# One attention-and-gate kernel: the order of its first loads and casts, and the queue of its output stores

## The chip, the cores and the metric

The kernel runs on one core of one Trainium2 chip. The metric is the device time of one execution in microseconds (us). Thirteen executions of the kernel before took 387.77 to 391.29 us, with a median of 389.75 us.

The engines are called as in the profile: PE is TensorE (PEld its weight loads), DVE is VectorE, ACT is ScalarE, POOL is GpSimd, and SP is SyncE, which only issues DMAs. DMAs issued by SP and ACT go to hardware queues (q1 and q10 in the profile), those issued by POOL to a software queue (q0).

## What is computed

```python
# q, k, v: (8 batches, 12 heads, 448 rows, 64), f32
scores = (1 / 8) * q @ k.T
m = max(scores); e = exp(scores - m)
x = (e / (sum(e) + exp(-m) + 1e-9)) @ v          # heads side by side: (8, 448, 768)
proj = x @ w_proj                                # (768, 2304), cut into x1, x2, x3
x2c = irfft(rfft(x2, axis=rows) * rfft(filter))  # filter: (448, 768)
out = (x1 * x2c * x3) @ w_out                    # (8, 448, 768), f32
```

The kernel computes in bf16 on PE. It leaves out the subtraction of the maximum, so that the denominator is the sum of exp plus 1, and it writes the two Fourier transforms as products with small cosine and sine tables.

## The kernel before

**Units of work.** Heads go in pairs: a batch has six pairs, and pair numbers run through the whole kernel. Pairs 0 to 5 are batch 0, pairs 6 to 11 batch 1, and so on to pair 47. Below, q8 is the query load of pair 8, k8 and v8 its key and value loads.

**Attention of a pair** (`attention`, from L650). Score products (L662 and L664) fill a PSUM tile `sc`, ACT takes the exponential of four tiles (L670 three times, L675 once), PE multiplies by the values in two halves (L707, L712), and DVE divides (L725 to L727) into `xb`. Then the result is turned, on PE in batches 0 and 1 (L761), into `xT`.

**The gate part of a batch** (`dense`) folds `xT` into `xf` on DVE (L822, L827), multiplies it by the middle third of `w_proj` (task P, L850), transforms it (task Z, L877), multiplies `xT` by the two other thirds (task G, L923), transforms back (task I, L962), and multiplies by `w_out` (task O, L1035). ACT copies each result of O into a ring of three tiles `osb` (L1047), and a DMA stores it (`store`, L1051). The filter's spectrum (L607, L614, L617, L624) is made once, in batch 0.

**How batches 0 and 1 get their inputs** (`staged`, L300). For each pair there is a key load, a value load and two query loads (one for each head), all f32, into one of four slots of `nat`. With them go four loads called rests, which hold the last 64 rows of keys and values of all heads. SP issues all of them but q0, in one order. A load must wait until the slot's last user has been cast. POOL casts to bf16: keys at L343, queries at L349, values at L356, rests at L372 and L377. Then PE turns keys and queries of the pair (L384 to L390; call this task T), and DVE, or ACT for pair 6, copies them into `kT` and `qT`. The casts of keys and queries write rings of two tiles, so that the key cast of pair 8, for example, must wait until T of pair 6 has run.

**How batches 2 to 7 get theirs** (`loaded`, L432). POOL issues DMAs that cast on the way (L441, L449, L451 and L463), and SP issues DMA transposes (L475, L480, and L751 for the attention's result).

**The weights and the filter** also come by POOL's software queue: the middle third of `w_proj` first, then the filter, the first third, the last third, and `w_out` (L555 to L559, L640, L645).

**What sets the order.** Nothing runs in the order of the code. Each step is a task with an engine, a cost, a due time, and the names of what it needs and makes. `Plan.run` plays the tasks through in a model of its own, and each engine always takes the most urgent task that is ready there. The program then holds the instructions of each engine in that order, and each engine runs them strictly in it. Three rules of the plan matter here:

- SP takes a load only if at most nine are under way with it; a query load counts as two (L128).
- A weight load becomes ready when the loads named in `GATES` (L210) have been issued, or their casts done. This exists in the plan alone: in the built program the first weight DMA waits for no semaphore and has only its place among POOL's instructions.
- The due times of values, rests and casts come from `tau`, which gives each pair of batch 0 a slot of 3.5.

The softmax here doesn't subtract the row's maximum and nothing guards it: scores larger than these inputs give would overflow.

## Time and profile before

| what | us |
|---|---|
| median of 13 executions (lowest to highest) | 389.75 (387.77 to 391.29) |
| the profiled execution's own time | 387.77 |
| its span, first to last instruction | 386.0 |
| PE busy in the span | 370.0 |
| DVE, ACT, POOL busy | 269.7, 264.3, 113.3 |
| moved by DMA | 50.44 MB, mean 131 GB/s |

Busy times are of one profiled execution. An engine's time without work counts only where the engine is the one that everything else waits for. The number after a group's x is how many instructions it has, and a bracket at a line's end says how long the engine was idle before it and what ended that.

The DMA queues of the profile count packets. For a load, a packet is one contiguous run: a query load's runs are 256 bytes, those of a key or value load 768 bytes.

### The profile page before, as it was taken

What the parts mean: (1) busy time and instruction counts of PE and PEld (TensorE: products, weight loads), DVE (VectorE), ACT (ScalarE), POOL (GpSimd) and SP (SyncE); (2) the same over time, 40 slices, a digit from 0 to 9 for tenths busy, and PEclk for the clock granted to TensorE, in tenths of its full rate; (3) what the DMA queues carried; (4) which work ended last, traced back from release to release, by engine and by line L of the source; (5) the groups of instructions that cost most, each with busy time, mean ns of one, the idle gap of its engine ahead of it and who ended that gap; (6) DMA issues with size and microseconds to landing.
All of it is one profiled execution on the core that took longest, in us unless ns stands there. A gap on an engine that the chain in (4) does not pass through costs nothing.

```text
span 386.0 us, 8977 instructions
## 1 busy us (share of the span) xinstructions
PE 370.0 (96%) x3461; PEld 232.7 (60%) x3461; DVE 269.7 (70%) x817; ACT 264.3 (68%) x460; POOL 113.3 (29%) x179
## 2 busy tenths in 40 slices
PE   6877999999999999999999999999999999999995
PEld 5554765656665566556756576556655566567652
DVE  6587669862987459956698439956699439964870
ACT  6788676737876757866877768766876758743543
POOL 7775828237241713331406222322100000000000
PEclk9899999999999999999999999999999999999999
DMA  8999999999999999799999699799951321012004
GB/s 202 244 251 230 213 206 176 149 123 226 145 141 126 221 163 137 88 110 167 149 119 87 145 171 136 88 107 160 120 70 30 122 56 29 15 54 84 0 2 164
DMA packets 179419, 50.44 MB, mean 131 GB/s; under 512 B 166125, under 2 KB 175792, under 8 KB 179376
## 3 DMA queue, kind: packets, MB, share of 16 engines
q0 software_dynamic: 101680, 17.80, 64.5%
q1 hardware_dynamic: 76768, 31.83, 42.5%
q8 instruction: 27, 0.44, 0.5%
q10 hardware_dynamic: 928, 0.23, 0.3%
q14 instruction: 16, 0.13, 0.1%
HBM read 43.86 MB, written 11.01 MB: 142 GB/s over the span
## 4 chain that ended last, share of the span: by engine, by line
PE 82%; DVE 7%; DMA 5%; ACT 2%; SPq 2%; issue 1%; POOL 0%; POOLq 0%
PE pps L923 24%; PE pps L850 15%; PE ops L1035 13%; PE op L712 8%; PE sc L662 7%; DMA wproj_bf<-in_moe_w_proj_dram 3%; PE op L707 3%; PE xsp L877 3%; PE cps L962 3%; DMA nat<-in_q_dram 2%; PE sc L664 2%; PE sc L923 1%; PE sc L850 1%; SPq L321 1%; DVE cv L991 1%
## 5 line engine op out<-in xcount | busy, mean ns | idle before, releaser
L670 ACT ACTIVATE e<-sc 128x896 bf16<-128x896 f32 x144 | 127.5, 923 | 17.2 <-PE sc L662 16.0
L923 PE MATMUL pps<-xT,wproj_bf 128*128 128x448 bf16 x522 | 110.6, 352 | 0.1
L923 PEld LDWEIGHTS <-wproj_bf 128*128 128x128 bf16 x576 | 52.0, 97 | 45.8 <-issue 5.9
L850 PE MATMUL pps<-wproj_bf,xf 128*113 128x384 bf16 x360 | 66.7, 328 | 1.0 <-DMA wproj_bf<-in_moe_w_proj_dram 0.8
L850 PEld LDWEIGHTS <-xf 128*113 128x113 bf16 x384 | 48.6, 132 | 16.4 <-issue 5.5
L712 PE MATMUL op<-vn,e 128*128 128x65 bf16 x1152 | 57.0, 194 | 0.0
L712 PEld LDWEIGHTS <-e 128*128 128x128 bf16 x1152 | 50.6, 98 | 5.2
L1035 PE MATMUL ops<-wout_bf,yT 128*128 128x384 bf16 x270 | 49.2, 326 | 0.1
L449 POOL DMA_DIRECT2D nat<-in_k_dram x36 | 29.8, 845 | 48.2 <-DMA kT<-nat 47.2
L727 DVE TENSOR_TENSOR xb<-op,rec 128x256 bf16<-128x256 f32 x96 | 40.7, 424 | 3.3
L707 PE MATMUL op<-vr,er 128*128 128x130 bf16 x192 | 42.2, 220 | 0.7 <-DVE xb L727 0.7
L725 DVE TENSOR_SCALAR rec<-op 128x4 f32<-128x4 f32 x96 | 15.2, 158 | 39.6 <-PE op L712 38.5
L662 PE MATMUL sc<-qT,kT 64*128 64x448 bf16 x288 | 40.9, 357 | 0.6 <-DVE qT L410 0.5
L1047 ACT COPY osb<-ops 128x384 f32<-128x384 f32 x52 | 24.2, 484 | 22.9 <-PE ops L1035 22.6
L1035 PEld LDWEIGHTS <-yT 128*128 128x128 bf16 x288 | 26.5, 98 | 20.0 <-DVE yT L1006 2.5
L891 DVE TENSOR_TENSOR t<-xs,hrs 113x768 bf16<-113x768 bf16 (+1 forms) x64 | 34.2, 552 | 5.6 <-ACT xs L885 5.4
L675 ACT ACTIVATE er<-sc 128x448 bf16<-128x448 f32 x48 | 26.7, 555 | 14.2 <-PE sc L664 13.5
L862 DVE CAST x<-pps 113x384 bf16<-113x384 f32 x32 | 17.7, 554 | 25.0 <-PE pps L850 24.9
L971 ACT CAST cr<-cps 128x452 bf16<-128x452 f32 x48 | 26.0, 550 | 9.4 <-PE cps L962 9.2
L938 DVE TENSOR_TENSOR g<-x,pps 128x448 bf16<-128x448 bf16 x45 | 27.8, 617 | 6.7 <-PE pps L923 6.4
L935 ACT CAST x<-pps 128x448 bf16<-128x448 f32 x42 | 23.0, 547 | 13.6 <-PE pps L923 12.6
L885 ACT CAST xs<-xsp 113x384 bf16<-113x384 f32 (+1 forms) x60 | 26.5, 490 | 3.8 <-PE xsp L877 3.2
(117 smaller groups left out, 463.7 us busy)
## 6 DMA issues: line engine op xcount, KB each, us to landing
out_dram<-osb SPq DMA_DIRECT2D x24, 384.0 KB, 2.4
nat<-in_q_dram POOLq DMA_DIRECT2D x24, 168.0 KB, 7.0
vn<-in_v_dram POOLq DMA_DIRECT2D x6, 672.0 KB, 11.0
wproj_bf<-in_moe_w_proj_dram POOLq DMA_DIRECT2D x3, 1152.0 KB, 12.1
nat<-in_k_dram POOLq DMA_DIRECT2D x36, 96.0 KB, 4.1
nat<-in_q_dram SPq DMA_DIRECT2D x22, 112.0 KB, 5.1
nat<-in_k_dram SPq DMA_DIRECT2D x12, 192.0 KB, 4.6
nat<-in_v_dram SPq DMA_DIRECT2D x12, 192.0 KB, 4.7
```

The lines of the kernel that those rows point to most:

```text
L449: nc.gpsimd.dma_start(kn[:, :, 1 + t, c], kr[:, :, 4 * u + t, :])
L662: nc.tensor.matmul(sc[:, u, 0:S], kT[b % 2][c, hp, t, :], qT[b % 2][c, hp, :])
L670: nc.scalar.activation(e[:, 0 : 2 * S].rearrange("p (u n) -> p u n", u=2), sc[:, :, 0:S], AF.Exp, scale=SCALE)
L675: nc.scalar.activation(e[:, 0:S], sc[:, 0, 0:S], AF.Exp, scale=SCALE)
L707: nc.tensor.matmul(op[:, n, :, :], e[0][:, o : o + 128], vr[b % 2][:, hp, :, :], start=True, stop=False)
L712: nc.tensor.matmul(op[:, n, u, :], e[1 + t][:, u * S + o : u * S + o + 128], vn[b % 2][:, hp, 4 * u + t, :], start=False, stop=(u == 1 and ...
L727: nc.vector.tensor_tensor(W["xb", b][:, hp, 2 * hf : 2 * hf + 2, :].rearrange("p t (u d) -> p t u d", u=2), op[:, :, :, 0:DH], rec[:].unsq ...
L850: nc.tensor.matmul(pps[:FQ, :DCH], W["xf", b][:, pg, kt, 0:FQ], wproj_bf[:, kt, D + ch * DCH : D + (ch + 1) * DCH], start=(kt == 0), stop= ...
L891: nc.vector.tensor_tensor(t[:K], L["xs", par, ch][:K], h, op=ALU.mult)
L923: nc.tensor.matmul(p[:, :S], wproj_bf[:, kt, 2 * part * D + dt * 128 : 2 * part * D + (dt + 1) * 128], xT()[:, kt, 0:S], start=(kt == 0), ...
L938: nc.vector.tensor_tensor(g[:, dt, :], L["x1", dt], p[:, :S], op=ALU.mult)
L1035: nc.tensor.matmul(ops[:n, :DCH], y[:, dt, 0:n], wout_bf[:, dt, ch * DCH : (ch + 1) * DCH], start=(dt == 0), stop=(dt == NDT - 1),)
```

## The change

Five edits of the plan's inputs, and one of the program:

1. The value loads of batch 0 are due 3.5 later in the plan (`VLATE`), and the rests of the values of batch 0 are due 0.4 later.
2. The two casts of batch 1's key rests are due 12.0 ahead of pair 6 instead of 5.9 (`CRK`).
3. The middle third of `w_proj` may be loaded once the keys and queries of pair 6 have been issued, where it was pair 7.
4. `REV` is a name for what was done already, and `late` is an argument that no task uses.
5. The output stores of batches 0 to 6 are issued by POOL on the software queue, not by SP. Those of batch 7 stay with SP. In the plan a store costs its engine 1.0, where it was 0.6.

```diff
+    VLATE = 3.5
+    CRK = 12.0
+    REV = True
...
     GATES = (
-        (1, [("iv", 5), ("ir", 1), ("ik", 7), ("iq", 7)]), ("F", [("cv", 8)]), (0, [("cv", 9)]), (2, [("cv", 10)]),
-        ("O", [("cv", 11)]),
+        (1, [("iv", 5), ("ir", 1), ("ik", 6), ("iq", 6)]), ("F", [("cv", 8)]), (0, [("cv", 9)]), (2, [("cv", 10)]), ("O", [("cv", 11)]),
     )
...
-                add("ACT" if first else "SP", 1.04 if name == "q" else 0.52, -21.0 if first else want + 0.1 * n, load, need=need,
+                add("ACT" if first else "SP", 1.04 if name == "q" else 0.52, -21.0 if first else want + 0.1 * n + (VLATE if name == "v" and b == 0 else 0.0), load, need=need,
...
-                    add("SP", 0.5, want + (0.05 if name == "k" else SLOT0 + 0.05) if b == 0 else want - RE1 + 0.1 * n,
+                    add("SP", 0.5, want + (0.05 if name == "k" else SLOT0 + 0.45) if b == 0 else want - RE1 + 0.1 * n,
...
-                    add("POOL" if on_pool else "DVE", 0.55 if on_pool else 0.37, tau(g) - 5.9 if g else 3.0,
+                    add("POOL" if on_pool else "DVE", 0.55 if on_pool else 0.37, tau(g) - CRK if g else 3.0,
...
+            dma = nc.sync if b == n_batches - 1 else nc.gpsimd
             if st < 3:
-                nc.sync.dma_start(out[b, st * 128 : (st + 1) * 128, :], osb)
+                dma.dma_start(out[b, st * 128 : (st + 1) * 128, :], osb)
                 return
             for i in range(1 + b % 2):
-                nc.sync.dma_start(out[b - b % 2 + i, 384:S, :], osb[i * REM : (i + 1) * REM])
+                dma.dma_start(out[b - b % 2 + i, 384:S, :], osb[i * REM : (i + 1) * REM])
...
-                add("SP", 0.6, w, lambda: store(st), need=[("os", b, st)], make=[("store", b, st)], give=[os_], dma=1.4, run=3072)
+                add("SP" if b == n_batches - 1 else "POOL", 1.0, w, lambda: store(st), need=[("os", b, st)], make=[("store", b, st)], give=[os_], dma=1.4, run=3072)
```

The numbers of the plan move the order of the built program. These are the first DMAs that SP issues, in both orders (k, v and r are one DMA each, q is two; rk and rv are rests, with the batch's number). The number in brackets is the place of the DMA before it.

```
before: k0 rk0 v0 k1 rv0 q1 v1 k2 q2 v2 k3 v3 q3 k4 v4 q4 rv1 rk1 k5 [23] q5 v5 v6 q6 k6 [30] v7 k7 q7 v8 k8 [36] q8 v9 k9 k10 [41] q9 v10 v11 q10 k11 q11
after:  k0 rk0 k1 q1 v0 rv0 k2 v1 q2 k3 q3 v2 k4 v3 rk1 q4 rv1 k5 v4 [23] k6 v5 k7 v6 q5 [29] v7 k8 k9 q6 v8 v9 [36] q7 v10 k10 v11 [41] q8 k11 q9 q10 q11
```

On POOL, the casts around the first weight load (w1 is the middle third, w0 the first) stand so:

```
before: ... k5 q5 v5 | w1 | q6 rk1 rk1 k6 v6 k7 rv1 rv1 v7 q7 v8 | filter | q8 k8 k9 v9 | w0 | ...
after:  ... k5 v4 k6 v5 | w1 | v6 q5 rv1 rv1 v7 rk1 rk1 k7 q6 k8 v8 | filter | q7 v9 | w0 | q8 k9 ...
```

On PE, T of pair 7 and the first score product of pair 7 move from before the first P to behind it; T of pair 6 moves from before the last scores of pair 5 to behind pair 5's value products; between the first P and T of pair 8 there were one P and one pair of scores, and now there are T of pair 7, two P and one pair of scores. After batch 1 PE's order is the same but for three swaps of neighbours. On POOL each store stands between the loads of a later batch: those of batch 2, for example, among the first key loads of batch 5, and those of batch 3 from the last query load of batch 6 on.

## Prediction

> **What bounds the kernel now.** First the page's slices for PE, then the busy time of each engine in four stretches (columns: stretch, length, busy time and instructions of PE, PEld, DVE, ACT, POOL, then granted clock, DMA share, GB/s).

> ```profile
> PE   6877999999999999999999999999999999999995
> ```
> ```profile
> 0.00:35.50 35.50, 26.38 (x349) 18.58 (x350) 25.56 (x88) 27.10 (x40) 25.36 (x73) 0.95 1.04 234
> 35.50:50.15 14.65, 14.37 (x138) 10.06 (x138) 9.26 (x25) 10.92 (x22) 8.72 (x15) 1.00 1.12 210
> 50.15:360.00 309.85, 308.42 (x2845) 192.34 (x2843) 221.90 (x672) 215.88 (x379) 79.19 (x92) 1.00 1.16 121
> ```

> PE idles 9.1 us of the first 35.5 and 1.7 of the next 324.5. So the time is the head, then PE's own work, which the change leaves as it is, then the tail. An edit gains only by an earlier first P (35.50), and loses wherever PE comes to wait after it. In the head DMA is busy throughout. The chain of waits (start, length, what) passes the head through query landings and the first weight:

> ```profile
> 17.30 3.33 DMA nat<-in_q_dram
> 21.97 1.42 issue
> 23.40 12.06 DMA wproj_bf<-in_moe_w_proj_dram
> ```

> The timeline of POOL shows w1's place and the gap ahead of it, and the filter; that of PE shows the first P, which waits 0.79 us for w1, and T of pairs 8 and 10:

> ```profile
> 21.32 0.64 POOL L356 CAST vn<-nat 128x192 bf16<-128x192 f32 x2
> 23.40 1.07 POOL L640 DMA_DIRECT2D wproj_bf<-in_moe_w_proj_dram  x1 [1.43 <-DMA nat<-in_q_dram]
> ...
> 31.09 0.75 POOL L555 DMA_DIRECT2D filt<-in_moe_filter_fft_dram  x1
> ```
> ```profile
> 35.50 1.14 PE L850 MATMUL pps<-wproj_bf,xf 128*113 128x384 bf16 x6 [0.79 <-DMA wproj_bf<-in_moe_w_proj_dram]
> ...
> 38.07 0.22 PE L384 MATMUL tps<-ident_bf,ks 128*128 128x128 bf16 x1
> ...
> 55.91 0.22 PE L384 MATMUL tps<-ident_bf,ks 128*128 128x128 bf16 x1
> ```

> Last the DMA queues (packets, MB, share), for 30 to 31 us, while w1 lands, and for 40 to 41, between two weights:

> ```profile
> q0 software_dynamic: 112, 0.17, 94.3%
> q1 hardware_dynamic: 110, 0.03, 21.2%
> ```
> ```profile
> q1 hardware_dynamic: 610, 0.22, 95.7%
> q0 software_dynamic: 11, 0.00, 3.2%
> ```

> While a weight lands, the two queues take turns packet by packet: SP's loads get 110 packets a us, and 600 where the software queue is empty. A query DMA is 448 packets of 256 bytes, so it takes 448 / 110 = 4.1 us beside a weight, a key or value DMA 256 / 110 = 2.3. This is the price that decides below. The trace agrees: the last three loads of the head, k11 and both parts of q11, landed at 47.62, 51.70 and 55.95, 4.1 and 4.3 apart, under w0 and w2.

> **The change part by part.** All sums stand against the profiled execution (387.77, the lowest of the 13; the median is 389.75). Differences are then put on the median.

> *Edits 1 to 3, the first P.* The casts ahead of w1 are now k5, v4, k6, v5. Their loads are SP's DMAs 22 to 25, and the landings at these places were 18.95, 19.61, 19.81 and 20.62. With casts of 0.50 and 0.64 (rows at 20.11 and 21.32) they end near 21.4. With the gap of 1.43 kept, w1 is issued at 22.8, 0.6 earlier. The gap's releaser is given as a query load, but the instruction waits for no semaphore in the program; if it is a wait that goes, w1 gains 2.0, if POOL is later, 0. P also needs the fold of batch 0. q5 now lands as DMA 28/29 (22.21 and 23.05 at these places) and is cast after w1's issue, near 25.2. Then come T of pair 5, six exponentials (0.45 to 0.92 each, some 4.7), the values and the fold: 35.6, where before it was 35.95. So the first P ends near 36.1, 0.5 earlier. T of pair 7 (0.42) and one score product (0.19) now stand behind it: together +0.1. If the fold does not follow, +0.6; if w1 gains 2.0 and the fold with it, -1.4.

> *Edits 1 and 3, the later queries.* SP's order in places 28 to 43 has the same kinds in the same places as before, so landings can be carried over by place. But places 42/43, which were q9, are now q8, and places 45/46 and 47/48, behind k11, are q9 and q10. Before, q8 landed at 35.13, q9 at 41.77 and q10 at 43.67, and T of pairs 8, 9 and 10 ran at 38.07, 49.98 and 55.91. So q9 and q10 had slack of 8 and 12 us; it is this slack that the change spends. Two more things take it. The filter's issue now stands behind the key cast of pair 8, which must wait for T of pair 6, and that stands behind the values of pair 5: near 33.5 instead of 31.09. And w0 is issued right after v9's cast, near 36.6, where it was 39.86. Before, the software queue was empty from about 39.5 to 42.5, and in that gap q9, v10, v11 and q10 all came through (41.77 to 43.67). After, filter, w0, w2 and wout follow each other without a gap.

> The slowest DMA engine sets a landing. Each DMA's semaphore gets 16 increments, one for each engine, and their times for place 40 are:

> ```
> 34.3 34.5 34.5 34.6 34.6 34.6 34.6 34.7 34.7 34.7 34.8 34.8 35.6 35.7 37.5 38.7
> ```

> Fourteen engines were through before the filter's packets came at 35.1, two lagged 1 to 2 us behind after w1 and took the rest at the slow rate. On the slowest, place 38 was through at 35.1 (an earlier w1 does not help: what it leaves sooner it took sooner). At the fast spacing of 0.6 a DMA places 39 to 43 would be through at 38.1. The filter's first packets come 4.0 us after its issue (31.09 to 35.1), so now at 37.5: one query DMA is left for the slow rate, and **q8 lands near 38.1 - 0.6 + 4.1 = 41.6**. The other bounds are the rows of w1 (23.40 to 26.6, 3.2 us) and w0 (39.86 to 42.3, 2.4): with 2.4, packets at 35.9, nearly four DMAs left, q8 near 48. From the other side, if no engine lags, q8 is through near 36.5.

> From there the queue has k11, q9 and q10 to bring: 2.3 + 4 x 4.2 = 19.1 us beside the weights. Hence q10 at 60.7, cast (0.61) at 61.3. PE would come to T of pair 10 at 55.9, so **PE loses 5.4 us**, of which 3.1 at T of pair 8 (41.6 + 0.6 against 39.1, where PE stands after P, T of pair 7, two P and two score products) and the rest at T of pair 10. For T of pair 11 two more query DMAs give 69.1, cast 69.7 against 64.15 + 5.4: the same within 0.2. Bounds: no lag, 36.5 + 19.1 + 0.6 - 55.9 = +0.3; late, the weights' own end stops it. Filter (5.9 long) and three weights of 8.2 (w0's 42.3 to 50.7 less its start) from 35.9 end near 66.5, and then the rest is fast: q10 near 66.5, loss 11. I take 4.0, since it is the filter's own row. POOL, SP and PE are in order, so what stands behind the stalls shifts by the same, and the loads of batch 2, which queue behind wout, with it.

> *Edits 2 and 4* cost nothing of their own: the two key-rest casts (0.53 each) stand on POOL ahead of the key cast of pair 8, which has to wait for T of pair 6 in any case, so POOL's wait there hides them. If that cover went, +1.

> *Edit 5, the stores.* Each issue now costs POOL 0.7 to 0.95 us (rows of L449 and L441), 27 of them in 240 us on an engine that is 29% busy; loads of later batches slip by 9 to 14 us, covered by a wait of 47.2 us that POOL has at L449 for the key transposes. What can be felt is `osb`: in batches 1, 3 and 5 a fourth copy needs the first store landed (batch 3: copied 213.59, store 213.61 to 216.44, fourth copy at 219.63). The page's rows:

> ```profile
> out_dram<-osb SPq DMA_DIRECT2D x24, 384.0 KB, 2.4
> ...
> nat<-in_q_dram POOLq DMA_DIRECT2D x24, 168.0 KB, 7.0
> ```

> At 2.4 there are 3.2 us in hand, at 7.0 the copy comes about 1.6 late, three times. So 0 to 4.8; since POOL's queue is empty in those places (its loads were done), I take 0.2.

> [...]

> **Sum:** 0.1 + 5.4 + 0.2 = +5.7, so 393.5 for the profiled execution and **395.4 on the median**.

> The stalls of 3 us leave PE without work, and the row of 12.0 to 15.4 shows the clock granted at 0.50 after an idle time of 1.08 us: by it up to 1.7 us more, which is within the upper bound. [...]

> **The rivals** (on the median).
> - *Later still* (0.22): the filter's packets come 2.4 to 3.2 us after issue; q8 lands at 44 to 48, loss 7 to 11, 397 to 401. The filter's own row speaks against it.
> - *Little lost* (0.20): the slow engines lag by less, or the filter is issued later than 33.5, so that q8 is through near 38 and q10 near 57: +0.5 to +3, 390.9 to 392.7. It decides from the filter's packets: after 38.1 at T of pair 8 nothing is lost.
> - *No change* (0.10): the same with no lag at all, 389 to 390.9.
> - *Faster* (0.20), the other side: the gap of 1.43 is a wait for a query load that goes; w1 gains 2.0, PE's half-clock stretch at 12.0 to 15.4 goes as well since T of pair 1 has its keys and queries sooner, and the whole fold comes 1.4 to 2 earlier, while q8 is in time for the reason just given: 387 to 388.4. It decides if q10 is cast by about 54.5. For it: the chain passes this gap; against it: a wait that no semaphore of the program holds.
> - The forecast (0.28): 393 to 397.

> A change that does nothing is excluded by the two orders.

> **How the numbers follow.** About 0.3% (1.2 us) can be told from no change. Faster 0.20; within 0.3%: the case of no change and a part of "little lost", 0.14; slower 0.66. Range: from the faster case's end at 388.2 to 399.5 in the later one, which leaves about 0.1 out on each side.

> **What would show it.** w1's issue near 22.8 and the first P at 34.9 to 35.5; the filter's issue near 33.5, its packets 4 us later; q8 landed near 41.6, q10 near 60.7; PE's lines for T of pairs 8 and 10 with waits of 2 to 3 us each, for a query cast of POOL; no such waits at L1047 in batches 1, 3 and 5. It is wrong if the two slow DMA engines are not slow there, if w0's packets leave a gap after the filter, or if P starts before 34.5.

## The result and the profile after

The changed kernel took **394.27 us** (median of 11 executions, 392.50 to 399.05), the kernel before 389.89 us (48 executions, 387.73 to 394.84): a ratio of **1.0117**, 95% interval 1.0096 to 1.0138, so 4.4 us slower. Ratios and intervals, here and below, are of the executions in the faster of two states alone (399.05 is of the slower), and so are not the quotients of the medians beside them. The prediction had 395.4. Its sign and its size held, but the places where the time goes are not the ones it named, as the profile shows.

The page of the changed kernel, the rows of PE and of the granted clock in 40 slices:

```profile
PE   7778989999999999999999999999999999999994
PEclk9986999999999999999999999999999999999999
```

The loss is again in the first slices, and the clock's row shows 8 and 6 there. The same three stretches as before (length, busy time of PE, PEld, DVE, ACT, POOL, then clock, DMA share, GB/s):

```profile
0.00:35.50 35.50, 27.44 (x327) 19.34 (x328) 24.92 (x83) 22.89 (x32) 22.12 (x66) 0.88 1.07 239
35.50:50.15 14.65, 13.11 (x126) 9.02 (x124) 10.75 (x24) 10.57 (x19) 9.81 (x20) 0.95 1.12 203
50.15:360.00 309.85, 306.44 (x2845) 189.69 (x2844) 220.22 (x670) 217.33 (x382) 95.70 (x120) 1.00 1.30 121
```

Read the counts in brackets, not the busy times: by 35.5 PE has run 327 matmuls where it had run 349. It was busy for longer (27.44 against 26.38) at a lower clock (0.88 against 0.95): in its trace a value matmul of L714 takes 246 ns (median) between 20.5 and 22.1 us, where the clock is 0.50, and 193 ns after 50 us, where it is 1.00. ACT did 8 instructions less and was busy 4.2 us less: it waited.

POOL's timeline answers to the lines of before. w1 is where it was (23.50), and the filter is 5.7 us later than before and 3.3 later than forecast:

```profile
23.50 1.05 POOL L642 DMA_DIRECT2D wproj_bf<-in_moe_w_proj_dram  x1 [1.98 <-issue]
...
25.13 0.62 POOL L351 CAST q<-nat 112x512 bf16<-112x512 f32 x1
...
35.78 0.51 POOL L345 CAST k<-nat 128x384 bf16<-128x384 f32 x1 [5.77 <-DVE xb L729]
36.23 0.64 POOL L358 CAST vn<-nat 128x192 bf16<-128x192 f32 x2
36.81 0.77 POOL L557 DMA_DIRECT2D filt<-in_moe_filter_fft_dram  x1
```

The key cast of pair 8 waits 5.77 us for T of pair 6, and the filter stands behind it. (The bracket names DVE's division, which ended within 0.02 us of T's last key product, at 35.74; in e1 the same wait names T: `POOL k L345 <- PE tps L388: 3.5, 1, 3.5`.) PE's timeline: the query part of T of pair 5, the first P in two pieces, T of pair 8 and T of pair 9.

```profile
25.81 0.37 PE L392 MATMUL tps<-ident_bf,q 112*128 112x112 bf16 x4
...
38.51 0.86 PE L852 MATMUL pps<-wproj_bf,xf 128*113 128x384 bf16 x4
40.02 0.53 PE L852 MATMUL pps<-wproj_bf,xf 128*113 128x384 bf16 x2 [0.65 <-DVE xf L829]
...
43.59 0.36 PE L392 MATMUL tps<-ident_bf,q 112*128 112x112 bf16 x4
...
54.83 0.22 PE L386 MATMUL tps<-ident_bf,ks 128*128 128x128 bf16 x1 [0.85 <-ACT xs L887]
...
56.14 1.14 PE L852 MATMUL pps<-wproj_bf,xf 128*113 128x384 bf16 x6 [0.40 <-ACT xs L887]
```

The first P ends at 40.55, where it ended at 36.64, and what it waits for is the fold (`xf`), no longer w1. T of pair 8 waits for nothing. T of pair 9 starts at 54.83 where it started at 49.98; in the kernel before, it and the P behind it stood so:

```profile
49.98 0.22 PE L384 MATMUL tps<-ident_bf,ks 128*128 128x128 bf16 x1
...
51.30 1.14 PE L850 MATMUL pps<-wproj_bf,xf 128*113 128x384 bf16 x6 [0.16 <-ACT xs L885]
```

**Where the 6.1 us of this profiled execution come from** (span 392.1 against 386.0). I matched PE's instructions one by one and took the difference of their starts. It is +3.9 at the end of the first P and +4.8 at T of pair 9, stays there until 100 us, and ends at +5.9 by 216 us, in steps of 0.2 to 0.6 with one of -0.7 at 135, where a wait of before is gone.

### The profile page after: what moved, and what is told of

Its sections match the earlier page's. It is cut to its first block, busy times and chain, and to the rows that moved or that the text cites. A ratio compares the mean times of both kernels' runs of the same rounds, so it can differ in the third digit from the quotient of the medians.

```text
span 392.1 us, 8976 instructions
## 1 busy us (share of the span) xinstructions
PE 373.7 (95%) x3461; PEld 234.4 (60%) x3461; DVE 272.2 (69%) x817; ACT 264.4 (67%) x460; POOL 127.6 (33%) x206
## 4 chain that ended last, share of the span: by engine, by line
PE 76%; DVE 11%; DMA 6%; ACT 3%; issue 2%; POOL 0%; SPq 0%; POOLq 0%; DVEq 0%
PE pps L925 20%; PE pps L852 14%; PE ops L1037 12%; PE op L714 8%; PE sc L664 7%; DMA xT<-xb 4%; PE op L709 3%; PE xsp L879 2%; PE sc L666 2%; PE cps L964 2%; DMA nat<-in_q_dram 2%; PE sc L925 1%; DVE cv L993 1%; DVE g L940 1%; PE spin L1116 1%
## 5 line engine op out<-in xcount | busy, mean ns | idle before, releaser
L1057 POOL DMA_DIRECT2D out_dram<-osb x21 | 11.9, 566 | 146.6 <-ACT osb L1049 134.9
L714 PE MATMUL op<-vn,e 128*128 128x65 bf16 x1152 | 59.0, 196 | 0.3 <-ACT e L672 0.2
L714 PEld LDWEIGHTS <-e 128*128 128x128 bf16 x1152 | 52.2, 99 | 6.2 <-ACT e L672 0.7
L727 DVE TENSOR_SCALAR rec<-op 128x4 f32<-128x4 f32 x96 | 15.2, 158 | 42.0 <-PE op L714 40.6
L1049 ACT COPY osb<-ops 128x384 f32<-128x384 f32 x52 | 24.1, 485 | 23.3 <-PE ops L1037 23.1
L893 DVE TENSOR_TENSOR t<-xs,hrs 113x768 bf16<-113x768 bf16 (+1 forms) x64 | 35.2, 567 | 3.5 <-ACT xs L887 3.3
## 6 DMA issues: line engine op xcount, KB each, us to landing
out_dram<-osb POOLq DMA_DIRECT2D x21, 384.0 KB, 2.9
nat<-in_q_dram POOLq DMA_DIRECT2D x24, 168.0 KB, 6.6
```

The lines of the kernel that those rows point to most:

```text
L714: nc.tensor.matmul(op[:, n, u, :], e[1 + t][:, u * S + o : u * S + o + 128], vn[b % 2][:, hp, 4 * u + t, :], start=False, stop=(u == 1 and ...
L893: nc.vector.tensor_tensor(t[:K], L["xs", par, ch][:K], h, op=ALU.mult)
```

## The experiments

Twelve kernels ran. Ratios are to the kernel before, on the same chip, in some 12 executions each unless said otherwise.

| kernel | median us | ratio, 95% interval |
|---|---|---|
| changed kernel | 394.27 | 1.0117 (1.0096 to 1.0138) |
| e1: stores back on SP | 392.03 | 1.0067 (1.0039 to 1.0095) |
| e2: edit 5 alone | 390.87 | 1.0038 (1.0008 to 1.0069) |
| e3: edit 1 alone (6 executions) | 393.84 | 1.0113 (1.0073 to 1.0154) |
| e4: edit 3 alone | 390.48 | 1.0019 (0.9986 to 1.0052) |
| e5: e1, query of pair 5 earlier | 391.87 | 1.0047 (1.0015 to 1.0078) |
| e6: e1, PE's wait at T of pair 4 filled | 392.89 | 1.0062 (1.0028 to 1.0096) |
| e7: before, PE's wait at T of pair 1 filled | 390.13 | 0.9997 (0.9964 to 1.0031) |
| e8: before, stores on ACT | 391.92 | 1.0026 (0.9996 to 1.0056) |

### e1 to e4: which part costs

Edit 2 needed no run: with it alone the order of every engine is that of before, and without it that of the changed kernel. e1 and e2 split the change at edit 5 (their head orders are exactly those of the changed kernel and of before). e3 and e4 take edits 1 and 3 alone.

```diff
# e1: the changed kernel, and in e2 the other way round
-            dma = nc.sync if b == n_batches - 1 else nc.gpsimd
+            dma = nc.sync
# e3 (the kernel before)          # e4 (the kernel before)
+    VLATE = 3.5                   -  ("ik", 7), ("iq", 7)
+    ... SLOT0 + 0.45              +  ("ik", 6), ("iq", 6)
```

> The changed kernel with edit 5 alone undone: all stores are back on SP, the head's order is that of the changed kernel. Theory A (the loss is in the head, in the new order of query loads and casts, and is there by the first P): stays near the changed kernel, +3.5 to +4.8 against before, first P near 38.5, the shift at T of pair 9 near +4.8. Rival B (the stores on the software queue delay copies and the loads of later batches): back to within 1 of before. The 1.1 that the changed kernel's trace gains after 130 us goes by B, and stays by A if it comes from the order alone.

Measured: +0.67%, 2.6 us. It is theory A's side, though under its band; the rest, 0.50% or about 1.9 us (uncertainty 0.35%, the two intervals added in squares), goes with the stores. PE's lines of e1 (T of pair 5, end of the first P, T of pair 9):

```profile
25.70 0.37 PE L392 MATMUL tps<-ident_bf,q 112*128 112x112 bf16 x4 [0.36 <-POOL q L351]
...
37.38 0.54 PE L852 MATMUL pps<-wproj_bf,xf 128*113 128x384 bf16 x2 [0.32 <-DVE xf L829]
...
52.20 0.22 PE L386 MATMUL tps<-ident_bf,ks 128*128 128x128 bf16 x1 [0.85 <-ACT xs L887]
```

The same order of the head gives a first P 2.6 us earlier than in the changed kernel's profile, still 1.3 later than before, and a T of pair 9 that is 2.2 later than before, not the 4.8 that theory A expected. So one profile of this head carries chance of some 2 us; medians decide. Over all traces the end of the first P spread from 36.4 to 38.2 with the old order of the head (before, e2, e7, e9) and from 37.9 to 40.6 with the new one (the changed kernel, e1, e6, e10, e11). Nor do the steps behind T of pair 9 show the part of the stores: from there to the end the changed kernel's trace loses another 1.1 us and that of e1, with the stores on SP, another 1.3.

> The kernel before with edit 5 alone: its PE, DVE and ACT orders are those of before, only SP's and POOL's differ behind batch 1. Theory A: 0 to +1.1 against before, no waits at the copies into osb. Rival B: +3 or more.

Measured: +0.38%, 1.5 us, a little over theory A's 1.1. No copy into `osb` waits for a store, as forecast. What waits is the fold. In e2's timeline DVE stands idle before a fold of batch 5, and PE, shortly after, for DVE:

```profile
244.10 0.17 DVE L821 COPY xT<-xT 128x6 bf16<-128x6 bf16 x1 [1.58 <-issue]
```
```profile
245.40 1.29 PE L925 MATMUL pps<-xT,wproj_bf 128*128 128x448 bf16 x6 [1.01 <-DVE g L940]
```

The fold needs a DMA transpose of `xb`, which landed at 244.03, 5.7 us after its issue; before, it took 3.9. In the DMA queues of e2 from 241 to 244 the software queue is full of query loads, in the kernel before (240.5 to 242.5) it is almost empty:

```profile
q0 software_dynamic: 1958, 0.25, 140.2%
q1 hardware_dynamic: 623, 0.15, 37.0%
```
```profile
q1 hardware_dynamic: 1518, 0.37, 120.1%
q0 software_dynamic: 76, 0.01, 7.3%
```

Those four loads were issued at 237.4 to 240.2, where before they went out at 230.2 to 234.2. The waits of the changed kernel name the reason and the effect (engine, what, for whom: us, times, longest):

```profile
POOL out_dram L1057 <- ACT osb L1049: 134.9, 18, 36.2
...
DVE xT L821 <- DMA xT<-xb: 2.2, 3, 1.0
```

POOL is in order. It stands at a store until ACT has made the tile, 134.9 us in all, and the loads behind the store go out late. That this costs the 1.5 us is argued from e2's trace and not shown: waits of the same form and size, for a fold and then on PE, stand also in traces with the stores on SP (159.07 and 160.37 in e1, 162.66 and 163.96 in e3, 158.52 and 159.81 in e4). Those of e1:

```profile
159.07 0.17 DVE L821 COPY xT<-xT 128x6 bf16<-128x6 bf16 x1 [1.59 <-issue]
```
```profile
160.37 0.92 PE L925 MATMUL pps<-xT,wproj_bf 128*128 128x448 bf16 x4 [0.85 <-DVE g L940]
```

> The kernel before with edit 1 alone: the loads in the changed kernel's order, but w1 issued only behind the casts of v6, value rests and q5. Theory A (the order of the query loads and what the clock makes of it): q5 cast some 1 us earlier than in the changed kernel (no weight issue ahead of it), w1 some 3 us later (issue near 26, landing near 38.5), first P near 38.5, +3 to +5. Rival (w1's place ahead of q5's cast is what costs): T of pair 5 near 24.4, the fold near 38, and no more than +2.

Measured: +1.13%, theory A's band; T of pair 5 at 25.50 also speaks against the rival. But its trace holds what I had forecast for the changed kernel. Here the filter goes out at 31.20 and the software queue is never empty after w1. SP's query loads in places 41 to 44 landed at 41.36, 45.17, 49.20 and 53.26: 3.8 to 4.1 us apart, the price of 4.1. The turn of pair 9 waits 2.05 us for its query cast at 54.08.

> The kernel before with edit 3 alone: the loads stay in their order, and w1 is issued ahead of the casts of k5, q5, v5 (near 20.5). Theory A: the query loads keep their places, so T of pair 5 comes only 1 us later, w1 lands near 33, first P bound by the fold at 35.5 to 36.5: -0.5 to +1. Rival (w1 ahead of the casts costs): software packets come sooner and slow q6 and q7, +2 or more.

Measured: +0.19%, no difference that can be told from none; theory A. Edit 1 alone has all of the head's loss, edit 3 alone none, and edit 2 does nothing: the head's loss comes from edit 1. That e1, with all three, shows less than e3 is within the intervals.

### e5: the query of pair 5 early

```diff
+ (VLATE if name == "v" and b == 0 else 0.0) - (3.5 if name == "q" and g == 5 else 0.0)
```

> The changed kernel with its stores on SP and the query load of pair 5 due 3.5 earlier, so that it stands ahead of k5 and is cast ahead of w1; values and weights stay late and early as the change has them. Theory A1 (what delays the first P is T of pair 5, 3.9 us later than before because q5 stands behind w1): T of pair 5 near 21.8 again, first P ends at 36 to 37, and the time falls from 392.0 to within 1 of before (389 to 391). Rival A2 (the clock's half-speed stretch after the idle time at T of pair 4 is what costs): the stretch stays and the time stays at 391.5 to 392.5.

Measured: +0.47%, 391.87, between the two. T of pair 5 is back at 21.57, and yet the first P starts at 38.35 in the profile. The wait has moved: now T of pair 7 stands ahead of the first P, and its query cast comes late.

```profile
37.01 0.55 PE L392 MATMUL tps<-ident_bf,q 112*128 112x112 bf16 x4 [1.94 <-POOL q L351]
```
```profile
36.34 0.61 POOL L351 CAST q<-nat 112x512 bf16<-112x512 f32 x1 [3.98 <-DMA nat<-in_q_dram]
```

q7's two halves landed at 33.42 and 36.22, over 10 us after their issue, beside w1. Theory A1 holds for T of pair 5 and fails for the time: the late query was not the only thing at its limit. (The profiled execution was the longest of e5's, 394.76 us, so its waits may be longer than those of most.)

### e6 and e7: the clock

30 matmuls ahead of T of pair 4 in e1, 18 ahead of T of pair 1 in the kernel before; T overwrites what they write.

```diff
+                for _ in range(FILL.get(g, 0)):
+                    nc.tensor.matmul(tps[:, 0:128], ident_bf, ident_bf)
```

> The changed kernel with its stores on SP and 30 matmuls of the identity by itself ahead of T of pair 4, whose result T overwrites: they take the 1.8 to 2.1 us in which PE waits for q4's cast. Theory A2 (clock): the granted clock stays at 1.00 from 20 to 23.4, values of pair 3 and 4 take half the time there, V of pair 4 ends 1 to 1.5 earlier; if that is what makes the first P late, 390.5 to 391. Theory A1: the clock stays up as well, but T of pair 5 still waits for q5's cast near 25.5, so the first P moves by less than 0.5 and the time stays near 392.

Measured: +0.62% (e1: +0.67%). The clock stayed at 1.00 from 20 to 24 and was then granted at half from 27.6 to 31, behind a wait of 1.84 for q5's cast, and again from 37.8 to 41.2; e1's trace had the one stretch, 20.1 to 23.5. Six value matmuls took 0.35 us at full clock (e6 from 20.1, e1 from 24.3) and 0.54 at half (e6 from 29.3, e1 from 20.4). No gain: theory A1's side. But as one stretch went and two came, this run doesn't price a stretch.

> The kernel before with 18 matmuls of the identity ahead of T of pair 1, where PE waits 1.08 us at 9.5. If the clock gate goes by PE's busy share in a window of 3.41 us (56% gated, 64% not), the half-speed stretch at 12.0 to 15.4 goes and the lowest times stay while the median falls by up to 1: 388.8 to 389.9. [...]

Measured: 0.9997. The profiled execution had the clock at 1.00 throughout, and the median granted clock of its 12 executions was 0.997 where that of the kernel before was 0.991. The stretches around T of pair 1, first of the kernel before, then of e7 (columns as above):

```profile
8.60:12.00 3.40, 1.94 (x28) 1.18 (x29) 1.57 (x6) 2.89 (x5) 2.94 (x8) 1.00 1.16 291
12.00:15.40 3.40, 3.40 (x36) 2.39 (x34) 2.55 (x9) 1.79 (x3) 1.99 (x6) 0.50 1.22 266
```
```profile
9.00:12.40 3.40, 2.71 (x44) 1.78 (x41) 1.55 (x7) 2.79 (x5) 3.21 (x9) 1.00 1.18 277
12.40:15.80 3.40, 2.86 (x41) 1.62 (x38) 2.73 (x11) 2.29 (x4) 2.56 (x8) 1.00 1.24 253
```

With the filler PE was busy for 2.71 us of the first stretch, not 1.94, the clock stayed up in the second, and the time did not follow. The half-speed stretch at T of pair 1 is, at the level of 0.3%, a mark of PE's waits and not a cost by itself. The other stretches were not tried so. Over 72 executions of the kernel before (those that e1 to e12 are held against), the 23 with a mean granted clock of 0.989 or less have a median of 390.44 us, the 29 with 0.993 or more one of 389.14: a lower clock and a longer time go together, and which makes which stays open. The 2 us by which the changed kernel's profile is worse than e1's go along with a second such stretch, but that they come from it is not shown.

### e8: stores on ACT

```diff
+            dma = nc.sync if b == n_batches - 1 else nc.scalar
```

> The kernel before with the stores of batches 0 to 6 issued by ACT, right behind the copies they need. Theory S1 (a store on POOL costs because POOL, in order, stands at it until the copy into osb is done, and the loads behind it then collide with the transposes of the attention's results): no wait of that kind here, loads of later batches as before, 389.5 to 390.5. Rival S2 (moving the stores off SP changes the transposes in any case, wherever they go): +1 or more, as with POOL; ACT's own issue work would add at most 24 x 0.6 spread over seven batches, off the path.

Measured: +0.26%, 0.9996 to 1.0056, which reaches into both bands. It does not tell S1 from S2; ACT's order also moved here. That the stores alone cost 0.1 to 0.7% on POOL's queue is measured, and the chain above is read from one trace; no run separates them.

### e9 to e12: the head by itself

Two batches only (`n_batches = 2`), 4 to 6 executions each. POOL's order is whole that of the full kernels, PE's for the first 142 tasks (137 in e11).

> The kernel before cut to batches 0 and 1 (batches 2 to 7 left out, their outputs are not written). POOL's order is whole that of before, PE's for its first 142 tasks (to some 95 us). It is the measure for the three beside it, as the loads of batch 2 and later cannot disturb it: some 115 to 130 us. The first P ends near 36.6, T of pair 9 near 50.

> The changed kernel's order of loads, casts and weights, cut to batches 0 and 1 in the same way. Theory A (the loss of 2 us comes in the head): +1.8 to +2.5 against the two-batch kernel before. Rival (it comes by later collisions with the loads of batch 2 and on): below +1.

> As the run before it, and one product P of batch 0 (third part, second half) moved behind the two transforms Z ahead of T of pair 9, where the kernel before had it. Theory B (1.1 of the loss is T of pair 9, which follows the two Z at once and waits for the PSUM bank that ACT's copy of Z gives back): the waits of 0.85 and 0.40 at T of pair 9 and at the P behind it fall to 0.2 in all, and the time falls by 0.9 to 1.1 against the changed head. Rival: the wait moves to another place, no change.

> Two batches, values of batch 0 a pair later as in the changed kernel, but the query loads of pairs 4 to 7 due 1.5 to 3.5 earlier, so that queries keep their old places and w1 is issued behind the casts of q5, k5 and v4. Theory A1 (late queries cost, not late values): T of pair 5 near 21.8, first P ends near 36.6, no wait at T of pair 7, and against the two-batch kernel before 0 to +1.1 (the wait at T of pair 9 stays). Rival A3 (the values come too late for the value products): PE waits ahead of values of pairs 2 to 5, +1.8 or more.

| two batches | median us | ratio to the full kernel before |
|---|---|---|
| e9: before | 126.07 | 0.3220 (0.3201 to 0.3238) |
| e10: changed head | 127.06 | 0.3259 (0.3243 to 0.3276) |
| e11: and P behind the two Z | 128.12 | 0.3281 (0.3263 to 0.3299) |
| e12: values late, queries early | 126.98 | 0.3236 (0.3215 to 0.3256) |

e10 less e9 is 0.0039 of 390, 1.5 us with an uncertainty of about 1 (the two intervals added in squares). That lies between the two bands, and the uncertainty reaches into both: the head's order costs something, and whether it is all of e1's 2.6 stays open. e11 refutes theory B in its form: T of pair 9 no longer waits, but P does in its place, for the same copies,

```profile
53.64 1.14 PE L852 MATMUL pps<-wproj_bf,xf 128*113 128x384 bf16 x6 [0.85 <-ACT xs L887]
```

and the time did not fall. Whatever follows the two Z waits; in the kernel before the same P stood there and did not. What differs ahead of them (the turn of pair 6's result directly before the two Z, where products of the filter's spectrum stood) may hold the third bank; that was not tried. e12 has T of pair 5 at 21.75, as forecast, but T of pair 6 at 27.88 with waits of 1.42 and 1.17 for POOL's casts of the key rests and keys, and a first P that ends at 39.1 (e9: 38.2). Its time is between e9 and e10 and told from neither. Chance between executions is in these places too: T of pair 9 stood at 52.15 in e9's trace, where the full kernel with the same order had 49.98.

## Why the prediction was right or wrong

**The sum was right to 1.3 us, and its largest term was wrong.** It had 0.1 for the first P, 5.4 for late queries at T of pairs 8 and 10, and 0.2 for the stores. Measured: nothing at T of pairs 8 and 10, about 2.6 (1.5 to 3.7 by e1's interval) for the head and what follows from its order, 1.5 to 1.9 for the stores. That the sum fits is luck: a term of 5.4 was not there, and two terms of 0.3 together came out at 4 or more.

*The first P* (forecast 0.5 earlier, and +0.1 with T of pair 7). w1's issue was put at 22.8 and came at 23.50 here and 22.92 in e1; q5's cast near 25.2 came at 25.13, T of pair 5 at 25.8. Up to there the working held. The step that failed is the next: I let "six exponentials, some 4.7" follow without a gap, so that the fold would be done at 35.6. In the timeline of ACT, first of the kernel before, then of the changed one, the exponentials at this place:

```profile
24.68 1.72 ACT L670 ACTIVATE e<-sc 128x896 bf16<-128x896 f32 x2
```
```profile
26.58 1.73 ACT L672 ACTIVATE e<-sc 128x896 bf16<-128x896 f32 x2 [1.20 <-PE sc L664]
29.31 0.54 ACT L677 ACTIVATE er<-sc 128x448 bf16<-128x448 f32 x1 [1.01 <-PE sc L666]
...
31.37 1.73 ACT L672 ACTIVATE e<-sc 128x896 bf16<-128x896 f32 x2 [0.71 <-PE sc L664]
...
37.04 0.56 ACT L770 COPY xT<-xps 128x448 bf16<-128x448 bf16 x1
```

ACT waited three times for scores, 2.9 us. The first wait (1.20) is for the last scores of pair 4, which stand on PE behind T of pair 5; the other two (1.01 and 0.71) are for scores of pair 5, which stand behind the turn of pair 3's result, where PE waited 0.81 and 0.46 us for DVE's division. Then T of pair 6 ran just ahead of the turn of pair 5's result, and ACT's copies for pair 6 (1.1 us) and of the filter's table (0.9) stood ahead of the copy of that result (37.04). This is the chain of the changed kernel's trace; in e1 the first of the three waits was 1.64, the second absent and the third 0.24, so its links shift from one execution to the next. A chain over four in-order engines can't be priced as the sum of its longest engine's work.

*The later queries* (forecast: q8 landed at 41.6, 3.1 lost at T of pair 8, the rest at T of pair 10). q8 landed at 38.92, and q9 and the first half of q10 by 40.42. The price of 4.1 us beside a weight is right, as e3 shows. What failed is "the filter's issue near 33.5": it took T of pair 6 from the first step. As pair 5 was late, so was T of pair 6, and the filter went out at 36.81. Its packets came from 38.2 to 39.0 on (a first one at 38.1), and so from 33.7 to 38.2 SP had the DMA engines to itself but for 28 packets. I had named this condition myself: "after 38.1 at T of pair 8 nothing is lost". The trace of the changed kernel at 37 to 38:

```profile
q1 hardware_dynamic: 680, 0.18, 88.0%
```

Before, it was 109 packets in that microsecond. Two steps hung on one time, the end of pair 5, and an error in it takes from the one what it adds to the other. In e1 the filter went out at 34.31, 0.8 later than forecast; its packets set in near 36.2 and were at their full rate only near 38, q8 landed at 38.67, and T of pair 8 lost nothing. There q9 and q10 did pay the price, with landings at 43.51, 47.17, 51.10 and 55.27, but T of pair 10 came at 58.12 and waited for nothing. One reading of the prediction is also wrong: it counts fourteen DMA engines through before 35.1, and its own list has twelve; on the slowest, place 38, which stood at 35.1 before, was through at 33.7 after the change.

*PE's order between the first P and T of pair 9* was taken as free. It cost 1.1 in every trace of this order (0.85 and 0.40 against 0.16), in waits that end with ACT's copy of Z. e11, which moved the P behind the two Z, did not get it back, so its cause is open.

*The stores* (0.2 of 0 to 4.8). The mechanism I priced, a fourth copy that waits for a landed store, never came. The one that came, as far as e2's trace shows it, loads pushed behind a waiting store on an in-order queue, I had seen as a slip of "9 to 14 us, covered by a wait of 47.2 us". The cover was for the loads' own users; that a load at another time collides with a transpose was not asked. In the changed kernel's trace the stores that POOL issued landed in 2.6 to 7.1 us, beside loads, with a median of 3.3. The half-clock term of 1.7, kept for the upper bound, is not borne out: by e7's interval the stretch at T of pair 1 cost at most 1.4 us.

## What to carry to other kernels

When one late event feeds two steps of an estimate, carry its error through both before adding them up. Where a chain crosses engines that run in order, list for each engine what stands ahead of the next link; only the sum over the links with those waits is a time. And before an instruction that must wait is put on an in-order queue, ask not only whether the work behind it has time, but what it meets when it starts later.

## What the runs showed of the hardware that was not expected

```
kernel before    8.58 to 11.99: 56% -> 0.50   29.06 to 32.47: 66% -> 1.00   32.47 to 35.88: 64% -> 1.00
changed kernel  16.59 to 20.00: 35% -> 0.50   26.83 to 30.24: 57% -> 0.50
from half speed 30.24 to 33.65: 85% -> 0.50   33.65 to 37.07: 88% -> 1.00
```

From 6.4 us on the clock of these two traces fell after the windows of 56, 35 and 57% listed here and after one of 16% and one of 0% at the ends of the spans. It stayed at 1.00 after all others; the lowest of those had 55% (385.2 to 388.6 in the changed kernel), 64, 66 and 67%. So 55% passed where 56 and 57% did not, and in these two traces the share alone does not tell which window is followed by half speed. From half speed the clock rose after windows of 100% (12.0 to 15.4 before, 20.0 to 23.4 after) and 88%, and stayed down after 85%. The longest single idle time in the two windows listed for the changed kernel is 2.1 us and 0.8 us; in the second of them PE was without work for 1.45 us in all, so short idle times alone stood ahead of that fall. By e7, the stretch at T of pair 1 cost nothing that could be measured (0.9997, interval 0.9964 to 1.0031).

The gap of 1.43 us ahead of w1, which the prediction's "faster" case took for a wait on a load, was 0.75 us in e1, 1.28 in e2, 1.52 in e6, 1.98 in the changed kernel and 3.32 in e5, and absent in e3 and e4, where w1 stands behind other casts. In the kernel before two packets of an instruction queue, of 0.3 to 0.4 us, stand at its edges (21.6 and 23.1); in the changed kernel two of 0.5 us start at 21.4 and 24.4. Whether they have to do with the gap is not shown.
